# Gradient tail of a recurrent-memory layer: FFN gradients placed between attention halves, memory blocks fetched ahead and turned in spread steps

## The chip, the cores and the metric

The kernel runs on one core of one Trainium2 chip. The metric is device time in microseconds (us) of one execution. Before the change three timed runs had a median of 3459.89 us (3448.79 to 3468.05). Engines are called as the profile calls them: TensorE or PE (matmuls and transposes), DVE and ACT (copies and packs), POOL and SP (here the two queues that issue transfers).

## The reference

A layer with two parts is run forward and backward: a recurrent attention, where 64 segments of 32 tokens pass 8 memory rows to one another, and a gated FFN. The outputs are the layer's result and nine gradients, all in bf16.

```python
h  = x + A(layernorm(x), mem0, Wq, Wk, Wv, Wo)    # 64 segments in sequence, 16 heads of 256
h2 = h + B(layernorm(h), w_gate, w_up, w_down)    # (silu(x w_gate) * (x w_up)) w_down
# returned: h2 and the gradients by x, mem0, Wq, Wk, Wv, Wo, w_gate, w_up, w_down
```

The kernel runs a forward chain, an FFN phase, a backward chain and then a **tail**, which multiplies stored activations with stored gradients to get the weight gradients. Only the tail is changed: first Wo (called O here), then six **units** for Wv, Wk, Wq by two halves (v0, v1, k0, k1, q0, q1), and DGP (w_gate), DU (w_up) and Z (w_down).

## The kernel before

Most of what the tail loads goes tile by tile into a ring of 33 slots of 4 KB per partition, handed out in turn:

```python
def ring():
    ri[0] += 1
    return slots[(ri[0] - 1) % len(slots)]
```

A unit needs 20 blocks of 128 rows. 16 are X tiles, loaded by transposing DMA on the queue of SP. 4 hold the memory rows: fetched on the queue of POOL into one buffer `ld`, packed by DVE and ACT into one buffer `pk`, turned by TensorE.

```python
def load_x(nm, hf):
    for t in range(NT):                         # 16
        x_t = ring()
        nc.sync.dma_start_transpose(out=x_t..., in_=dr["X_" + nm][t]...)
def load_m(nm, hf):
    for g in range(NG):                         # 4
        nc.gpsimd.dma_start(out=ld, in_=dr["M_" + nm]...)
        nc.vector.tensor_copy(out=pk[:, 0:8], in_=ld...)
        nc.scalar.copy(out=pk[:, 8:16], in_=ld...)
        x_t = ring()
        for q in range(2):                      # 8 transposes each, then k.evac(x_t...)
            ...
```

A unit makes two passes over its 20 blocks; the next unit's memory blocks are made in one go between them.

```python
nxt = load_m("v", 0)
for hi, (nm, oi, hf) in enumerate(halves):
    xt = load_x(nm, hf)
    xt.update(nxt)
    for q in range(2):
        d_by_e(lambda b: HC[:, b, :], rhs, NB, (512, 512), st)
        if q == 0 and hi + 1 < len(halves):
            nxt = load_m(halves[hi + 1][0], halves[hi + 1][2])
GO = A(0, NB, D)                                # takes the place of HC
# load GO; then DGP, then DU, then Z (the only one that reads GO)
```

HC, HN and GO are operands kept whole outside the ring: HC for the six units, HN for DGP and DU, GO (the gradient of the output) for Z.

## Time and profile before

| stretch of the trace before | us |
|---|---|
| before the tail | 2713.3 |
| O | 135.0 |
| six attention units, DGP, DU | 530.3 |
| Z and the end | 50.9 |
| the tail, from O's first matmul on | 716.2 |
| span | 3429.5 |

Each stretch begins with the first matmul of its part. "Z and the end" begins with the start of the last matmul before Z, so that a wait of Z counts to Z. The view of who waited for whom, TensorE alone, over the six units (columns: engine, tile and line, what it waited for; us in total, times, longest):

```profile
PE ph L925 <- DVE arA L919: 15.5, 11, 6.5
PE psf L945 <- DMA arW<-X_k: 7.1, 4, 2.8
PE psf L945 <- DMA arW<-X_v: 4.1, 3, 1.7
PE psf L945 <- DMA arW<-X_q: 2.1, 2, 1.6
PE psf L945 <- DMA arA<-X_k: 1.2, 2, 0.7
PE psf L945 <- DMA arA<-X_q: 1.0, 1, 1.0
```

The first row is the wait of the transposes for a pack, the other five (15.5 us too) are waits for X tiles. Together 31.0 us.

### The profile page before, as it was taken

How to read it: one execution, taken by the hardware profiler on the slowest of the kernel's cores; microseconds unless marked ns; L12 is line 12 of the kernel's file. 1: busy time of each engine (PE TensorE's matmuls, PEld its weight loads, DVE VectorE, ACT ScalarE, POOL GpSimd, SP SyncE). 2: the span in 40 equal slices, each digit the busy share in tenths (PEclk: the TensorE clock that was granted, in tenths of full speed). 3: DMA queues.
4: the chain of work that ended last, by engine and by line, in shares of the span. 5: the costliest groups of instructions: out<-in, count | busy, mean ns of one | idle time of the engine just before them, and what ended most of it. 6: DMA issues, size and time to landing. Idle time of an engine off the chain costs nothing.

```text
span 3429.5 us, 120857 instructions
## 1 busy us (share of the span) xinstructions
PE 3044.6 (89%) x55036; PEld 2058.0 (60%) x55046; DVE 1308.3 (38%) x2912; ACT 971.0 (28%) x2171; POOL 616.2 (18%) x1293
## 2 busy tenths in 40 slices
PE   5999999999999578882999999999999899999999
PEld 4777777777777355661666666666666454443444
DVE  4444444444444256670444444444444201111101
ACT  1333333333333223330333333333333202111100
POOL 2111111111111111111122121212221111111111
PEclk8999999999999899995999999999999899999999
DMA  7545433644544787899688777878787969888571
GB/s 263 155 133 149 155 125 128 174 136 131 148 139 134 196 189 176 185 210 229 142 159 178 164 168 157 177 161 165 166 177 163 308 195 209 175 173 173 155 249 38
DMA packets 994213, 583.65 MB, mean 170 GB/s; under 512 B 904564, under 2 KB 913108, under 8 KB 992100
## 3 DMA queue, kind: packets, MB, share of 16 engines
q1 hardware_dynamic: 925748, 340.37, 47.6%
q0 software_dynamic: 67952, 235.56, 20.6%
q8 instruction: 430, 7.05, 0.9%
q14 instruction: 83, 0.68, 0.1%
HBM read 104.05 MB, written 250.19 MB: 103 GB/s over the span
## 4 chain that ended last, share of the span: by engine, by line
PE 61%; issue 13%; DMA 10%; DVE 8%; SPq 4%; ACT 2%; POOL 2%; ACTq 0%; DVEq 0%; POOLq 0%
PE psf L385 12%; PE po L780 7%; PE psf L422 5%; PE psf L737 5%; PE psf L945 4%; PE psf L715 4%; PE po L460 3%; PE fx L486 3%; PE fx L839 3%; PE psf L560 2%; SPq L910 2%; PE psf L802 2%; DVE arA L75 2%; PE psf L469 2%; DMA arW<-in_A_Wo_dram 2%
## 5 line engine op out<-in xcount | busy, mean ns | idle before, releaser
L77 ACT CAST arA<-psf 128x320 bf16<-128x320 f32 (+4 forms) x1139 | 487.0, 447 | 1611.8 <-PE psf L385 449.5
L75 DVE CAST arA<-psf 128x384 bf16<-128x384 f32 (+6 forms) x1029 | 491.7, 495 | 1085.1 <-PE psf L945 363.3
L385 PE MATMUL psf<-arA,arW 128*128 128x40 bf16 x16384 | 434.9, 181 | 34.3 <-issue 13.1
L385 PEld LDWEIGHTS <-arW 128*128 128x128 bf16 x16384 | 432.7, 97 | 49.6 <-issue 26.9
L780 PE MATMUL po<-arW,arA 128*32 128x448 bf16 x6144 | 355.2, 362 | 46.9 <-DMA arW<-in_A_Wv_dram 25.5
L737 PE MATMUL psf<-arA,arW 128*128 128x40 bf16 x8192 | 219.6, 180 | 51.3 <-POOL arA L672 41.1
L945 PE MATMUL psf<-arW,arA 128*128 128x512 bf16 x990 | 252.7, 383 | 13.4 <-DMA arW<-X_k 7.1
L422 PE MATMUL psf<-arW,arA 128*64 128x512 bf16 x2048 | 260.5, 383 | 2.4 <-DMA arW<-in_A_Wv_dram 2.4
L737 PEld LDWEIGHTS <-arW 128*128 128x128 bf16 x8192 | 215.3, 96 | 71.1 <-issue 70.6
L780 PEld LDWEIGHTS <-arA 128*32 128x32 bf16 x6144 | 155.2, 98 | 163.1 <-issue 35.2
L945 PEld LDWEIGHTS <-arA 128*128 128x128 bf16 x1440 | 135.4, 98 | 189.3 <-issue 44.7
L560 PE MATMUL psf<-arA,arW 128*128 128x256 bf16 x1344 | 166.1, 286 | 82.3 <-DMA arA<-arA 48.6
L560 PEld LDWEIGHTS <-arW 128*128 128x128 bf16 x1344 | 137.3, 102 | 113.5 <-issue 85.8
L422 PEld LDWEIGHTS <-arA 128*64 128x64 bf16 x2048 | 147.2, 111 | 70.3 <-issue 3.5
L75 DVE CAST arB<-psf 40x320 bf16<-40x320 f32 x320 | 107.7, 336 | 98.7 <-PE psf L451 65.0
L715 PEld LDWEIGHTS <-arW 128*128 128x128 bf16 x2048 | 87.9, 101 | 66.4 <-issue 62.7
L77 ACT CAST arB<-psf 128x96 bf16<-128x96 f32 (+1 forms) x320 | 98.2, 307 | 104.2 <-DVE arB L75 51.7
L486 PE MATMUL fx<-arW,arA 128*128 128x448 bf16 x512 | 124.5, 353 | 0.0
L747 ACT COPY arA<-psf 128x1024 bf16<-128x1024 bf16 x128 | 123.4, 1015 | 3.2 <-PE psf L746 1.7
L460 PE MATMUL po<-arW,arB 128*8 128x448 bf16 x2048 | 110.8, 359 | 9.0 <-DMA arW<-in_A_Wo_dram 5.4
L715 PE MATMUL psf<-arB,arW 128*128 128x80 bf16 x2048 | 98.7, 203 | 17.3 <-DVE arB L764 7.7
L966 PE MATMUL psf<-arW 128*128 128x448 bf16 x450 | 95.4, 361 | 5.8 <-DMA arW<-X_o 5.7
(238 smaller groups left out, 3741.8 us busy)
## 6 DMA issues: line engine op xcount, KB each, us to landing
QT<-arA POOLq DMA_DIRECT2D x64, 512.0 KB, 4.1
KT<-arA SPq DMA_DIRECT2D x64, 512.0 KB, 3.4
VG<-arA SPq DMA_DIRECT2D x64, 512.0 KB, 3.1
X_o<-arA POOLq DMA_DIRECT2D x40, 512.0 KB, 4.3
X_v<-arA POOLq DMA_DIRECT2D x32, 512.0 KB, 6.5
X_k<-arA POOLq DMA_DIRECT2D x32, 512.0 KB, 4.0
X_q<-arA POOLq DMA_DIRECT2D x32, 512.0 KB, 4.3
arW<-X_o SPq DMA_DIRECT2D x30, 512.0 KB, 13.7
```

The costliest lines, as they stand in the source:

```text
L75: nc.vector.tensor_copy(out=out, in_=in_)
L77: nc.scalar.copy(out=out, in_=in_)
L385: nc.tensor.matmul(pss[b][:, jj * L:(jj + 1) * L], lhsT=W_sb[:, kc, c * P:(c + 1) * P], rhs=hT_roll[:, kc, sl, :], start=(kc == 0), stop=( ...
L422: nc.tensor.matmul(pV[b][64 * g:64 * g + 64, 0:512], lhsT=hT_flat[:, kc, sl * L:sl * L + 64], rhs=Wv_sb[:, kc, n * 512:(n + 1) * 512], sta ...
L460: nc.tensor.matmul(pO[32 * (j % 4):32 * (j % 4) + M, 0:D], lhsT=o8[:, j, :], rhs=Wo_sb[:, cj(j), :], start=(j < 4), stop=(j >= MC - 4), sk ...
L486: nc.tensor.matmul(px[:, 0:D], lhsT=xblk[:, j, :], rhs=Wo_sb[:, cj(j), :], start=(j == 0), stop=(j == MC - 1))
L560: nc.tensor.matmul(ps[:, f2 * 256:(f2 + 1) * 256], lhsT=Wt[:, kc, c * P:(c + 1) * P], rhs=xT[:, kc, :], start=(kc == 0), stop=(kc == KC - 1))
L715: nc.tensor.matmul(ps[b][:, i * 2 * L:(i + 1) * 2 * L], lhsT=lhs[:, cl, :], rhs=rhs_bd[:, cl // 2, :, :].rearrange("p g n -> p (g n)"), st ...
L737: nc.tensor.matmul(pss[b][:, jj * L:(jj + 1) * L], lhsT=WoT_sb[:, kc, c * P:(c + 1) * P], rhs=do_roll[:, kc, sl, :], start=(kc == 0), stop ...
L747: nc.scalar.copy(out=dO_sb[:, 8 * hf:8 * hf + 8, :], in_=ph.rearrange("p (c n) -> p c n", n=P))
L780: nc.tensor.matmul(pH[32 * (j % 4):32 * (j % 4) + 32, 0:D], lhsT=blk[nm][:, j, r * SEG:(r + 1) * SEG], rhs=WT[:, cj(j), :], start=(nm == " ...
L945: nc.tensor.matmul(pa[2 * kc + g][:, 0:w], lhsT=lhs_of(b)[:, kc * P:(kc + 1) * P], rhs=rhs_of(b, g), start=(b == 0), stop=(b == nblk - 1), ...
```

## The change

Its intent is that TensorE never waits in the units. (1) Two `ld` and two `pk` buffers. (2) Fetch, pack and turn become separate steps, hung into the unit's own first pass four blocks apart, with two fetches in the pass before. (3) DGP after v0 and DU after k0. (4) A unit's X tiles now take their slots before its memory blocks; this follows from (2). In the cut below f, p and t with a number are the fetch, the pack and the turn of memory block 0 to 3.

```diff
-    ld = A(33.5, 4, 16, 32)
-    pk = A(37.5, 16, 4, 32)
+    ld_b = [A(33.5, 4, 16, 32), B(0, 4, 16, 32)]
+    pk_b = [A(37.5, 16, 4, 32), B(4, 16, 4, 32)]
...  load_m now returns a list of (fetch, pack, turn); in d_by_e:
         for b0 in range(0, nblk, 4):
+            for fn in (at or {}).get(b0, ()):
+                fn()
...  in att(hi, mem, after):
         xt = load_x(nm, hf)
-        xt.update(nxt)
+        for g in range(NG):
+            xt[NT + g] = ring()
...
+            if q == 0:
+                at = {0: [p0, f2], 4: [lambda: t0(xt[NT]), p1, f3], 8: [lambda: t1(xt[NT + 1]), p2],
+                      12: [lambda: t2(xt[NT + 2]), p3], 16: [lambda: t3(xt[NT + 3])]}
+            elif after is not None:
+                at = {12: [after[0][0], after[1][0]]}
...
+    for hi in range(len(halves)):
+        att(hi, mems[hi], mems[hi + 1] if hi not in (0, 2) else None)
+        if hi == 0:
+            up_grad("DGP", 7, mems[1])
+        if hi == 2:
+            up_grad("DU", 8, mems[3])
+    GO = A(0, NB, D)          # loaded here, and Z follows at once
```

More of the change, by code (lines that the diff above doesn't have):

```diff
@@ L914, in load_m, with fetch, pack, turn @@
     def load_m(nm, hf):
-        tiles = {}
+        todo = []
         for g in range(NG):
-            nc.gpsimd.dma_start(out=ld, in_=dr["M_" + nm][g * 4:(g + 1) * 4].rearrange(
-                "s p (c m) -> p s c m", m=32)[:, :, hf * 16:(hf + 1) * 16, :])
-            nc.vector.tensor_copy(out=pk[:, 0:8], in_=ld[:, :, 0:8, :].rearrange("p s c m -> p c s m"))
-            nc.scalar.copy(out=pk[:, 8:16], in_=ld[:, :, 8:16, :].rearrange("p s c m -> p c s m"))
-            x_t = ring()
-            for q in range(2):
-                pt = k.ph1()
-                for i in range(8):
-                    nc.tensor.transpose(pt[:, i * P:(i + 1) * P], pk[:, 8 * q + i].rearrange("p s m -> p (s m)"), ident[:, :])
-                k.evac(x_t[:, q * 1024:(q + 1) * 1024], pt[:, 0:1024])
-            tiles[NT + g] = x_t
-        return tiles
+            def fetch(g=g, ld=ld_b[g % 2]):
+                nc.gpsimd.dma_start(out=ld, in_=dr["M_" + nm][g * 4:(g + 1) * 4].rearrange(
+                    "s p (c m) -> p s c m", m=32)[:, :, hf * 16:(hf + 1) * 16, :])
+            def pack(ld=ld_b[g % 2], pk=pk_b[g % 2]):
+                nc.vector.tensor_copy(out=pk[:, 0:8], in_=ld[:, :, 0:8, :].rearrange("p s c m -> p c s m"))
+                nc.scalar.copy(out=pk[:, 8:16], in_=ld[:, :, 8:16, :].rearrange("p s c m -> p c s m"))
+            def turn(x_t, pk=pk_b[g % 2]):
+                for q in range(2):
+                    pt = k.ph1()
+                    for i in range(8):
+                        nc.tensor.transpose(pt[:, i * P:(i + 1) * P], pk[:, 8 * q + i].rearrange("p s m -> p (s m)"), ident[:, :])
+                    k.evac(x_t[:, q * 1024:(q + 1) * 1024], pt[:, 0:1024])
+            todo.append((fetch, pack, turn))
+        return todo
     dcs = dr["DHb"].rearrange("(t p) d -> p t d", p=P)[:, :, 0:D]
@@ L935, in tail_phase, with d_by_e @@
     nc.gpsimd.dma_start(out=HC, in_=dr["HC"].rearrange("(t p) d -> p t d", p=P)[:, :, 0:D])
-    def d_by_e(lhs_of, rhs_of, nblk, widths, store):
+    def d_by_e(lhs_of, rhs_of, nblk, widths, store, at=None):
         pa = accs(7)
         for b0 in range(0, nblk, 4):
+            for fn in (at or {}).get(b0, ()):
+                fn()
             for b in range(b0, min(nblk, b0 + 4)):
@@ L985, in tail_phase, with att @@
     halves = [(nm, oi, hf) for (nm, oi) in (("v", 5), ("k", 4), ("q", 3)) for hf in range(2)]
-    nxt = load_m("v", 0)
-    for hi, (nm, oi, hf) in enumerate(halves):
+    def att(hi, mem, after):
+        nm, oi, hf = halves[hi]
         o2 = OUT[oi].rearrange("d h e -> d (h e)")
         xt = load_x(nm, hf)
-        xt.update(nxt)
+        for g in range(NG):
+            xt[NT + g] = ring()
         for q in range(2):
+            at = {}
+            if q == 0:
+                (f0, p0, t0), (f1, p1, t1), (f2, p2, t2), (f3, p3, t3) = mem
+                at = {0: [p0, f2], 4: [lambda: t0(xt[NT]), p1, f3], 8: [lambda: t1(xt[NT + 1]), p2],
+                      12: [lambda: t2(xt[NT + 2]), p3], 16: [lambda: t3(xt[NT + 3])]}
+            elif after is not None:
+                at = {12: [after[0][0], after[1][0]]}
             def st(kc, g, r, q=q, hf=hf, o2=o2):
@@ L997, in rhs, with up_grad @@
                 return xt[b].rearrange("p (cl g n) -> p cl g n", g=2, n=P)[:, 4 * q:4 * q + 4, g, :]
-            d_by_e(lambda b: HC[:, b, :], rhs, NB, (512, 512), st)
-            if q == 0 and hi + 1 < len(halves):
-                nxt = load_m(halves[hi + 1][0], halves[hi + 1][2])
-        if hi == 1:
-            nc.gpsimd.dma_start(out=HN[:, 0:NT, :], in_=dr["HN"].rearrange("(t p) d -> p t d", p=P))
-    GO = A(0, NB, D)
-    nc.gpsimd.dma_start(out=GO[:, 0:NT, :], in_=GO2.rearrange("(t p) d -> p t d", p=P))
-    for (nm, oi) in (("DGP", 7), ("DU", 8)):
+            d_by_e(lambda b: HC[:, b, :], rhs, NB, (512, 512), st, at)
+    def up_grad(nm, oi, after):
         xt = []
@@ L1020, in rhs @@
                 return xt[b][:, p0 + 512 * g:p0 + 512 * g + ws[g]]
-            d_by_e(lambda b: HN[:, b, :], rhs, NT, ws, st)
+            d_by_e(lambda b: HN[:, b, :], rhs, NT, ws, st, {8: [after[0][0], after[1][0]]} if p0 else None)
+    mems = [load_m(nm, hf) for (nm, _, hf) in halves] + [None]
+    mems[0][0][0]()
+    mems[0][1][0]()
+    for hi in range(len(halves)):
+        att(hi, mems[hi], mems[hi + 1] if hi not in (0, 2) else None)
+        if hi == 0:
+            nc.gpsimd.dma_start(out=HN[:, 0:NT, :], in_=dr["HN"].rearrange("(t p) d -> p t d", p=P))
+            up_grad("DGP", 7, mems[1])
+        if hi == 2:
+            up_grad("DU", 8, mems[3])
+    GO = A(0, NB, D)
+    nc.gpsimd.dma_start(out=GO[:, 0:NT, :], in_=GO2.rearrange("(t p) d -> p t d", p=P))
     zt = []
```

## The prediction

> **What bounds the kernel now.** The change touches only the tail, the last phase, which computes the weight gradients. So I first asked how much of the run the tail is, then how much of it is TensorE idling. The page (its heading, and its first part) gives the scale:
>
> ```profile
> span 3429.5 us, 120857 instructions
> PE 3044.6 (89%) x55036; PEld 2058.0 (60%) x55046; DVE 1308.3 (38%) x2912; ACT 971.0 (28%) x2171; POOL 616.2 (18%) x1293
> ```
>
> TensorE leads. The groups by line put the attention part of the tail (L925, L945, L950) from 2847.8 to 3288.9 us; then come the two FFN gradients (DGP, DU) to 3378 and the Z gradient to 3421.5. Everything before 2847.8, 83% of the run, keeps its code.
>
> The attention part is six units (v, k, q by two halves), each of two passes over 20 blocks. From the timeline of TensorE, four blocks are 24 matmuls of 512 columns every 0.2157 us (5.18 us) and eight narrow ones in 1.05 us: 6.27 us in steady state. A pass is five of these, 31.35 us. The turning of one unit's memory blocks is 64 transposes, eight in 0.45 us: 3.6 us. I cut the busy-time view at the pass borders (columns: stretch, its length, PE, PEld, DVE, ACT, POOL busy with counts, clock, DMA share, GB/s):
>
> ```profile
> 2847.80:2892.05 44.25, 37.75 (x225) 17.67 (x224) 6.98 (x13) 10.61 (x14) 6.67 (x11) 0.92 1.12 230
> 2930.08:2966.03 35.95, 31.81 (x162) 13.13 (x162) 2.57 (x4) 2.15 (x4) 4.27 (x9) 1.00 0.72 132
> 2966.03:3003.84 37.81, 35.94 (x225) 16.71 (x226) 6.85 (x12) 10.27 (x12) 7.48 (x13) 1.00 0.91 203
> 3077.70:3116.09 38.39, 34.29 (x162) 13.70 (x163) 2.57 (x4) 2.14 (x4) 4.27 (x9) 0.91 0.72 136
> 3226.30:3257.60 31.30, 31.30 (x161) 13.13 (x160) 2.57 (x4) 2.14 (x4) 4.24 (x9) 1.00 0.48 98
> ```
>
> The last pass shows the ideal, 31.3. Passes with transposes (counts of 225) should take 34.95. The twelve passes took 44.25, 38.03, 35.95, 37.81, 36.03, 37.83, 38.39, 37.81, 35.00, 37.40, 31.30 and 31.40: together 441.1 us, against 12 x 31.35 + 6 x 3.6 = 397.8. So 43.3 us are lost, and that is all this part has to give.
>
> There are two losers, and they fall in different passes. The six passes with transposes lose 9.3 + 3.1 + 2.9 + 2.9 + 2.9 + 2.4 = 23.4 us; four passes without them lose 4.6 + 4.7 + 7.0 + 3.6 = 19.9 us. The chain that ended last (start, length, what), in one of the first kind:
>
> ```profile
> 2969.05 1.06 ACT arA L920
> 2970.39 3.90 DMA arA<-M_k
> 2974.37 1.05 ACT arA L920
> 2975.71 4.43 DMA arA<-M_k
> 2980.23 0.44 DVE arA L919
> 2980.72 0.62 PE ph L925 x8
> ```
>
> One buffer holds the fetched block: the next fetch starts only after ACT has packed the last one, and four rounds of fetch (about 4 us) and pack (1 us) run in series while PE, which takes its instructions in order, has come to the transposes.
>
> For the second kind, the timeline of the queue of SP, which loads the X tiles (start, length of the run of issues, what):
>
> ```profile
> 2901.98 6.36 SPq L910 DMA_TRANSPOSE arW<-X_v  x2
> 2911.28 29.31 SPq L910 DMA_TRANSPOSE arW<-X_k  x9
> 2940.76 9.84 SPq L910 DMA_TRANSPOSE arW<-X_v  x4
> ```
>
> Unit v1 starts at 2930.1 and needs its last four X_v tiles by block 12, but nine tiles of the unit after it go first. The chain runs through these SP issues and a 5.66 us landing until 2951. I read the cause in the code: the ring has 33 slots, a unit takes 4 (memory blocks) and then 16 (X), so X tiles 9 to 12 of the next unit inherit the slots of this unit's memory blocks, read last of all. The tiles of the unit after that inherit slots free earlier and overtake. The last unit has no such loss: after it come plain, quick row loads.
>
> **What the Trainium skill says.** "Perfetto Trace Analysis", section Optimization Strategy, says that where the most-contended engine changes between regimes, interleaving them can help. The trace agrees that the regimes differ: DMA share is 0.72 to 1.12 in the stalled passes, 0.26 in DU and 0.12 in Z. "TensorE: Matmul & The Clock Gate", section Part 1, says an idle window of about 3.4 us halves the clock until some 3.4 us of work. The trace agrees in kind: after the 6.48 us wait at 2855.98 eight transposes took 1.03 us instead of 0.61, and the 10 us around it had a clock of 0.66. "DMA: Bandwidth & Descriptors", section Latency and other measured facts, gives DMA transposes 261 GB/s; 512 KB would be 2.0 us, my estimate, and the shortest issue in the trace is 2.03. Its section on issuing engines says that SP and POOL queues share the same 16 engines; the median M fetch takes 4.6 us to land but up to 14.9 in a full queue.
>
> **The change part by part.** No matmul, transpose, copy or byte is added or removed. The work of 397.8 + 89 (DGP and DU) + 43.5 (Z) us stays.
>
> 1. Memory blocks. There are two fetch and two pack buffers; blocks 0 and 1 are fetched at block 12 of the preceding pass, two groups of 6.3 us ahead; block 2 right after the first pack. Each fetch has about 12.5 us before its pack, which has 6.3 us before its transposes. Against 4.6 us to land and 1.05 us to pack, the wait goes. Of 23.4 us I leave 3: 2 for the first unit, whose fetches meet other loads, 1 for the rest. Gain 20.
>
> 2. Ring order and placement. X tiles now take slots before the memory blocks, so slots are handed on in the order in which they are read and nothing overtakes. Placing DGP after v0 and DU after k0 gives 44 us of PE work with light loads (16 plain row tiles of 448 KB) just where 16 transposes must arrive. With 13 slots ahead of a 20-slot unit, 13 X tiles of the next unit can start while this unit starts. At an observed 2.8 to 3.2 us each, 16 take about 50 us, inside a unit of 66.3. Of 19.9 us I leave 3. Gain 17.
>
> 3. New cost: the GO load. It overwrites HC, so it waits for the last attention unit's blocks 0 to 15, ends 6.3 us before that unit, and Z now follows at once (before, DGP and DU lay between). Its row in the view by source line:
>
> ```profile
> L1005 POOL DMA_DIRECT2D arA<-in_grad_out_dram x1: 1199/1199/1199, 3283.0 to 3283.0; - x1
> DMA to landing us min/median/max: 14.0/14.0/14.0
> ```
>
> Those 14 us were beside 15 DU loads (DMA share 0.92 to 1.02). The same-sized HN load took 9.9 us. With Zt already in, I take 9 to 10: PE waits about 3.5 us. Cost 3.5.
>
> 4. Everything else, 0: HN has 66 us of slack before DGP; the end after the last matmul (8 us) is unchanged.
>
> Sum: 20 + 17 - 3.5 = 33.5 us, 1.0% of 3459.89. Predicted: 3426 us.
>
> **Rivals.**
> - *GO becomes a real stall.* If it lands in 14 us again, PE idles 7.7 us and restarts at half clock, some 2 to 3 us more: about 3433. For it: 1.8 MB in one transfer with one completion. Against it: the DMA queue is nearly empty there.
> - *DMA is the true bound*, so the X waits only move. A pass pair 2930 to 3004 holds 35.95 x 0.72 + 37.81 x 0.91 = 60.3 us of DMA work, 91% of 66.3. If loads slip in k1, q0 and q1, which have no light part between them, 8 to 12 us of part 2 come back: about 3437. Against it: the share falls below 0.3 in 10 us slices of every such unit, so the limit was order and not rate.
> - *The queue order at build turns out badly.* Order on each engine is fixed and differs from the program's (transposes sit between matmuls now). If a pack or a fetch is placed where POOL or DVE waits on something late, stalls return: 3450 to 3470. A new overtaking on SP would do the same. Nothing in the profile shows it; the slack of 12 us speaks against it.
> - *Nothing remains at all*: both residues zero and GO hidden: 3417.
>
> **Range and chances.** The most there is to win is 43.3 us, 1.25%, so faster by over 2% would need time from phases the change does not touch. Slower by over 2% needs 69 us of new waits. The three times before spread from 3448.8 to 3468.1, so I add some 8 us of noise either way to 3417 to 3440: range 3408 to 3446. Chances: 0.02 faster, 0.96 same, 0.02 slower.
>
> **What would show it right or wrong.** Right: twelve attention passes near 31.4 or 35 us; no M fetch in the chain inside them; on SP no tile of a later unit ahead of an earlier unit's; DGP and DU still 44 to 45 us each; PE idle 2 to 5 us before the first Z matmul, waiting for the gradient-output load; a span shorter by about 33 us. Wrong: waits on X in units k1, q0 and q1 (DMA rate was the bound), waits of PE on packs (placement), or a Z wait over 7 us. A changed time before 2847.8 would mean that the earlier phases had moved, which I put at zero.

## The result

The changed kernel had a median of 3404.42 us (3398.78 to 3418.66, 4 runs), the kernel before 3454.92 (3448.79 to 3468.05, 4 runs). The ratio is 0.9855, 95% interval 0.9809 to 0.9901. (A ratio is the mean time of one kernel's runs over that of the other's of the same rounds, so not quite the ratio of the medians.) Within 2%, as forecast; but 3404.42 lies just under the forecast range of 3408 to 3446.

The profile after, heading and first part:

```profile
span 3397.0 us, 120843 instructions
PE 3040.2 (89%) x55036; PEld 2058.9 (61%) x55046; DVE 1307.9 (39%) x2912; ACT 969.1 (29%) x2171; POOL 615.3 (18%) x1293
```

The span is 32.5 us shorter than before with the same counts of matmuls and copies: no work went, only idle time. Who waited, TensorE alone, from the first unit to the end:

```profile
PE psf L972 <- DMA arA<-in_grad_out_dram: 5.4, 1, 5.4
PE psf L951 <- issue: 0.3, 2, 0.2
```

All six rows of before are gone and a new one stands there. The ends of the passes, read from DVE's evacuations (timeline of DVE; start, length, what, idle before it and its releaser):

```profile
3062.20 1.89 DVE L75 CAST arA<-psf 128x512 bf16<-128x512 f32 x3 [3.65 <-issue]
...
3093.55 1.89 DVE L75 CAST arA<-psf 128x512 bf16<-128x512 f32 x3 [28.60 <-PE psf L951]
...
3118.63 1.89 DVE L75 CAST arA<-psf 128x512 bf16<-128x512 f32 x3 [22.33 <-PE psf L951]
...
3138.90 1.88 DVE L75 CAST arA<-psf 128x512 bf16<-128x512 f32 x3 [17.52 <-PE psf L951]
```

From 3062.20 to 3093.55 is k0's second pass: 31.35 us, the ideal to the hundredth. The next two distances, 25.08 and 20.27, are DU's passes, and passes with transposes from v1 on take 34.9 to 35.2. Units, DGP and DU together took 489.3 us against an ideal of 12 x 31.35 + 6 x 3.6 + 2 x 45.35 = 488.5. SP's timeline shows the loads in unit order:

```profile
2892.99 47.45 SPq L910 DMA_TRANSPOSE arW<-X_v  x16
2947.42 9.02 SPq L910 DMA_TRANSPOSE arA<-X_k  x3
...
3088.65 29.45 SPq L910 DMA_TRANSPOSE arW<-X_k  x10
3125.62 26.37 SPq L910 DMA_TRANSPOSE arW<-X_q  x9
```

No X tile stands before one of an earlier unit. The new cost, before Z (timeline of TensorE):

```profile
3339.26 1.05 PE L956 MATMUL fx<-arW,arA 128*64 128x512 bf16 x8
3345.66 2.03 PE L972 MATMUL psf<-arA,arW 128*128 128x448 bf16 x5 [5.35 <-DMA arA<-in_grad_out_dram]
```

The same place in the trace of before, then POOL after the change:

```profile
3378.93 1.12 PE L966 MATMUL psf<-arA,arW 128*128 128x448 bf16 x5
```

```profile
3336.32 1.20 POOL L1045 DMA_DIRECT2D arA<-in_grad_out_dram  x1 [24.06 <-issue]
```

GO landed 9.2 us after its issue began. TensorE stood still for 5.35 us, and its first five matmuls took 2.03 us where five took 1.12 at the same place before. Z and the end grew from 50.9 to 57.1 us.

By stretch, after: 2714.2 before the tail, O 136.4, units with DGP and DU 489.3, Z and the end 57.1; tail 682.8. The tail is 33.4 us shorter. The forecast sum was 33.5. The medians of the timed runs differ by 50.5, though, and the experiments had to find out which of the two is the gain.

### The profile page after: what moved, and what is told of

It is laid out like the page before. It is cut to its first block, busy times and chain, and to the rows that moved or that the text cites.

```text
span 3397.0 us, 120843 instructions
## 1 busy us (share of the span) xinstructions
PE 3040.2 (89%) x55036; PEld 2058.9 (61%) x55046; DVE 1307.9 (39%) x2912; ACT 969.1 (29%) x2171; POOL 615.3 (18%) x1293
## 4 chain that ended last, share of the span: by engine, by line
PE 71%; DMA 8%; issue 8%; DVE 8%; SPq 2%; ACT 2%; POOL 1%; DVEq 0%; ACTq 0%; POOLq 0%
PE psf L385 12%; PE psf L951 8%; PE po L780 7%; PE psf L422 6%; PE psf L737 5%; PE psf L715 4%; PE po L460 3%; PE fx L486 3%; PE psf L972 3%; PE fx L839 3%; PE psf L560 3%; PE psf L802 2%; PE fx L956 2%; PE psf L469 2%; DVE arA L75 2%
## 5 line engine op out<-in xcount | busy, mean ns | idle before, releaser
L75 DVE CAST arA<-psf 128x384 bf16<-128x384 f32 (+6 forms) x1029 | 492.1, 495 | 1007.7 <-PE psf L385 322.8
L385 PEld LDWEIGHTS <-arW 128*128 128x128 bf16 x16384 | 432.2, 97 | 48.9 <-issue 26.5
L737 PEld LDWEIGHTS <-arW 128*128 128x128 bf16 x8192 | 216.2, 97 | 71.9 <-issue 71.5
L951 PE MATMUL psf<-arW,arA 128*128 128x512 bf16 x1030 | 259.5, 379 | 0.0
L951 PEld LDWEIGHTS <-arA 128*128 128x128 bf16 x1440 | 136.0, 98 | 164.8 <-issue 13.7
L560 PEld LDWEIGHTS <-arW 128*128 128x128 bf16 x1344 | 139.0, 104 | 113.3 <-issue 83.3
L75 DVE CAST arB<-psf 40x320 bf16<-40x320 f32 x320 | 107.8, 337 | 98.2 <-PE psf L451 65.0
L715 PEld LDWEIGHTS <-arW 128*128 128x128 bf16 x2048 | 88.0, 101 | 66.4 <-issue 63.5
L972 PEld LDWEIGHTS <-arW 128*128 128x128 bf16 x606 | 59.4, 100 | 76.0 <-DMA arW<-X_o 13.3
```

Of the source, the lines that this page charges most:

```text
L75: nc.vector.tensor_copy(out=out, in_=in_)
L385: nc.tensor.matmul(pss[b][:, jj * L:(jj + 1) * L], lhsT=W_sb[:, kc, c * P:(c + 1) * P], rhs=hT_roll[:, kc, sl, :], start=(kc == 0), stop=( ...
L560: nc.tensor.matmul(ps[:, f2 * 256:(f2 + 1) * 256], lhsT=Wt[:, kc, c * P:(c + 1) * P], rhs=xT[:, kc, :], start=(kc == 0), stop=(kc == KC - 1))
L715: nc.tensor.matmul(ps[b][:, i * 2 * L:(i + 1) * 2 * L], lhsT=lhs[:, cl, :], rhs=rhs_bd[:, cl // 2, :, :].rearrange("p g n -> p (g n)"), st ...
L737: nc.tensor.matmul(pss[b][:, jj * L:(jj + 1) * L], lhsT=WoT_sb[:, kc, c * P:(c + 1) * P], rhs=do_roll[:, kc, sl, :], start=(kc == 0), stop ...
L951: nc.tensor.matmul(pa[2 * kc + g][:, 0:w], lhsT=lhs_of(b)[:, kc * P:(kc + 1) * P], rhs=rhs_of(b, g), start=(b == 0), stop=(b == nblk - 1), ...
```

## Experiments

Twelve runs. A trace's tail is measured as above. This table has all of it; "pack" and "loads" are TensorE's waits in the units in that trace.

| run | median us | ratio to before (95%) | before the tail | units, DGP, DU | Z, end | tail | pack | loads |
|---|---|---|---|---|---|---|---|---|
| before, first trace | 3459.89 | | 2713.3 | 530.3 | 50.9 | 716.2 | 15.5 | 15.5 |
| before_again | 3441.63 | 1.0004 (0.9969-1.0040) | 2736.0 | 526.5 | 50.9 | 712.0 | 14.0 | 15.0 |
| before_third | 3434.78 | 0.9975 (0.9942-1.0008) | 2703.6 | 530.3 | 50.9 | 716.6 | 17.1 | 15.7 |
| changed, first trace | 3404.42 | 0.9855 (0.9809-0.9901) | 2714.2 | 489.3 | 57.1 | 682.8 | 0 | 0 |
| after_again | 3412.66 | 0.9928 (0.9890-0.9965) | 2721.1 | 489.3 | 57.8 | 686.0 | 0 | 0 |
| after_third | 3417.52 | 0.9920 (0.9886-0.9954) | 2739.2 | 489.2 | 57.1 | 682.1 | 0 | 0 |
| go_early | 3404.32 | 0.9889 (0.9851-0.9927) | 2729.2 | 489.3 | 50.8 | 677.9 | 0 | 0 |
| steps_only | 3405.28 | 0.9892 (0.9858-0.9925) | 2723.1 | 489.2 | 50.1 | 675.2 | 0 | 0 |
| steps_one | 3407.70 | 0.9885 (0.9848-0.9921) | 2726.0 | 499.6 | 50.4 | 684.7 | 0.5 | 0 |
| one_buffer | 3408.54 | 0.9890 (0.9826-0.9953) | 2720.8 | 489.3 | 53.7 | 678.1 | 0 | 0 |
| old_order | 3438.39 | 0.9975 (0.9914-1.0036) | 2728.7 | 519.8 | 50.1 | 706.7 | 0 | 22.5 |
| placed_only | 3452.20 | 1.0000 (0.9932-1.0068) | 2729.8 | 528.2 | 58.6 | 721.4 | 24.8 | 3.7 |
| ring_order (wrong results) | 3448.47 | 0.9988 (0.9913-1.0063) | 2740.9 | 533.8 | 50.9 | 719.6 | 20.9 | 0 |
| own_unit | 3452.71 | 1.0023 (0.9989-1.0056) | 2733.9 | 541.2 | 50.4 | 726.3 | 36.1 | 0 |

Two things can be read off at once. The column "before the tail" runs from 2703.6 to 2740.9 though that code is the same in every row. The column "tail" repeats within 4.6 us for the same kernel.

### How large is the gain? before_again, after_again, after_third, before_third

Edit: none.

> The kernel before, unchanged, against itself. It tests the question that the forecast left: the two profiles differ by 32.5 us, the medians of the timed runs by 50.5 us. Theory N (scatter of the phases before the tail, whose code is the same): ratio 1.000 with an interval that reaches at least 0.3% to either side, and in this second trace the tail (first matmul of the output-weight gradient to the end of the span) again takes 716 us within 3 us, with any difference of the span lying before it. Rival S (the tail of the kernel before is itself slower in most runs than in the one profile that I read, because its loads come late by luck): the tail in this trace is 5 us or more over 716, with more waits for X or M tiles.

> The changed kernel, unchanged, timed in five rounds. Theory N: the gain is that of the two profiles' tails, 716.2 - 682.8 = 33.4 us, ratio 0.990 within 0.002, tail again 683 us within 2 us. Rival S: the ratio stays at 0.985 to 0.987 and the tail of the kernel before is the longer by some 50 us.

> The changed kernel a third time, beside the smaller version in the same rounds. Theory N (the difference of the tails is the whole gain): tail 683 to 686, ratio to before 0.990 within 0.003, 5 to 9 us above the smaller version. The stretch from the end of the forward chain to the end of the FFN's matmuls, whose code no version changes, scatters again between 389 and 417 us.

> The kernel before, a third trace. Theory N: tail 712 to 717; everything else that differs lies in the same stretch of the FFN. Rival Y (the kernel before is slower there too, for a reason that the change removes): this trace has that stretch over 405 us and the third trace of the changed kernel has it under 400.

Most of the scatter lies before the tail. Against itself the kernel before gave 1.0004 and 0.9975. Its three tails were 716.2, 712.0 and 716.6, mean 714.9; those of the changed kernel 682.8, 686.0 and 682.1, mean 683.6. The difference is 31.3 us. My bounds were a little narrow: 712.0, 686.0 and 682.1 lie about 1 us outside them, and so does the ratio of after_again (0.9928, forecast 0.988 to 0.992). The forecast for after_third also missed in its last part: its tail was 2.6 us below that of the smaller version (steps_one), not 5 to 9 above. The stretch from the end of the forward chain to the end of the FFN's matmuls took 389.2 us in the first trace of before and 416.7 in the second. The busy-time view over just that stretch, first before_again, then before_third (391 us there):

```profile
1149.30:1566.00 416.70, 303.45 (x2185) 209.99 (x2182) 232.10 (x352) 112.44 (x196) 66.97 (x122) 0.88 0.89 185
```

```profile
1149.00:1540.00 391.00, 305.32 (x2183) 210.56 (x2180) 232.00 (x352) 112.53 (x195) 67.34 (x122) 0.90 0.88 197
```

Every engine's busy time agrees within 2 us; 25.7 us of idling differ. Most of it is one wait of the FFN's first matmuls for a DMA, at most 61.8 us in before_again against 44.0 in before_third:

```profile
PE psf L560 <- DMA arA<-arA: 68.1, 6, 61.8
```

```profile
PE psf L560 <- DMA arA<-arA: 47.3, 4, 44.0
```

Rival Y, that the kernel before is slower there as well, falls: its third trace had 391.0 in this stretch and the changed kernel's third had 411.0. In the fourteen traces this one wait took 42.0 to 61.8 us: 43.7, 61.8 and 44.0 in the kernel before, 42.0, 56.0 and 59.7 in the changed one. Why that transfer varies from run to run was not tried. The three ratios of the changed kernel, 0.9855, 0.9928 and 0.9920, have a mean of 0.9901, which is 34 us of the mean of before (45 runs on several chips: 3444.2 us, from 3421.9 to 3470.4, standard deviation 11.7). The mean of the changed kernel's 16 runs is 3414.3, 29.9 less. Timed runs and traced tails agree on 30 to 34 us, 0.9 to 1.0%.

### Is the wait for GO a cost with nothing behind it? go_early

```diff
         if hi == 2:
             up_grad("DU", 8, mems[3])
+            GO = W(0, NB, D)              # in the place of HN, which nothing reads after DU
+            # load GO here
-    GO = A(0, NB, D)
-    # load GO here
```

> The changed kernel with the gradient-output block put in the place of HN instead of HC, and loaded right after the DU gradient, so that Z need not wait for it. Theory (the 5.4 us wait before Z is a new cost of the change and has nothing behind it): that wait is 0, the slow-clock restart of Z (about 2 us more) is gone too, the tail is 7 us shorter than the changed kernel's 683, about 676, and the time 0.2% below the changed kernel's. Rival (the Zt loads or the PSUM hand-over wait as long behind it): the wait changes its name and the tail stays within 2 us of 683.

The wait is gone, Z and the end took 50.8 us again, and the tail was 677.9, which is 5.7 under the changed kernel's mean of 683.6 (forecast 7; O was 1.4 us longer here than in the first trace of the change). Nothing stood behind that wait.

### Does the placement earn anything? steps_only and placed_only

steps_only is the changed kernel with DGP and DU moved back behind the units:

```diff
-        att(hi, mems[hi], mems[hi + 1] if hi not in (0, 2) else None)
-        if hi == 0:
-            up_grad("DGP", 7, mems[1])
-        if hi == 2:
-            up_grad("DU", 8, mems[3])
+        att(hi, mems[hi], mems[hi + 1])
     GO = A(0, NB, D)
+    # load GO, then up_grad("DGP", 7), up_grad("DU", 8)
```

> The changed kernel without the placement: all six attention units first, then DGP, DU and Z as before; two buffers, spread steps and the new slot order stay. Theory O (the order in which ring slots are handed on was the cause of the X waits, and placement adds nothing): no X wait over 1 us in total, and, as the gradient-output load is hidden again behind DU, a tail 5 to 8 us shorter than the changed kernel's, about 676. Rival P (the light FFN loads between the units are what lets the X tiles arrive): X waits of 10 to 20 us return and the tail is 690 to 700.

Theory O held: no load was waited for, the units with DGP and DU took 489.2 us, and with GO hidden behind DGP again the tail was 675.2. So with the new slot order and the spread steps the placement earns nothing and costs the wait for GO.

placed_only is the kernel before with the placement alone; during DGP and DU the memory blocks for the next unit are made between their passes.

```diff
         for q in range(2):
             d_by_e(...)
-            if q == 0 and hi + 1 < len(halves):
+            if q == 0 and hi in (1, 3, 4):
                 nxt = load_m(...)
+        if hi == 0:
+            nxt = up_grad("DGP", 7, ("v", 1))     # load_m after its first pass
+        if hi == 2:
+            nxt = up_grad("DU", 8, ("k", 1))
```

> The kernel before with the placement alone: DGP after v0 and DU after k0, the next unit's memory blocks fetched, packed and turned in one go between the two passes of whatever comes before it, one buffer each, memory slots still ahead of X slots. In the queue of SP as built, three DGP tiles come after twelve X_v tiles and the last four X_k tiles of k0 come after thirteen DU tiles. Theory O: overtaking is only moved, X and FFN tile waits of 8 to 15 us stay, pack waits of 12 to 16 us stay, and the wait for the gradient-output block before Z (5 us and 2 of restart) is added: tail 712 to 722, no gain. Rival P (placement helps by itself): loads wait under 5 us, tail under 706.

The tail (721.4) fell in the range of Theory O, but not for its reason. The waits in this trace from the first unit to the end:

```profile
PE ph L925 <- DVE arA L919: 24.8, 12, 7.5
PE psf L966 <- DMA arA<-in_grad_out_dram: 6.3, 1, 6.3
PE psf L945 <- DMA arW<-X_q: 3.7, 3, 1.6
```

Placement does cure most of the X waits (3.7 us instead of 15), as Rival P said. But the waits for packs rose from about 15 to 24.8 and took nearly all of it back: the units with DGP and DU took 528.2 us against a mean of 529.0 before. What made the tail 6.5 us longer than before is the wait for GO (Z and the end 58.6 us instead of 50.9). M_v fetches landed at a median of 8.6 us instead of 6.0; the two that grew most were issued at 2880.5 and 2890.3 us, beside the plain rows of DGP. What made them late was not tested.

### The two waits one at a time: ring_order, own_unit and old_order

ring_order was to be the new slot order alone:

```diff
+    slot = [ring() for _ in range(NB)]            # 16 for X, then 4 for memory, ahead of each unit
-            x_t = ring()                          # in load_x
+            x_t = got[t]
-            x_t = ring()                          # in load_m
+            x_t = got[NT + g]
```

> The kernel before with one thing changed: a unit's ring slots are handed out to its 16 X tiles first and to its 4 memory blocks after them. Buffers, steps and placement are those of before. In the queue of SP as built, no tile of a later unit now stands before one of an earlier unit. Theory O (handing on of slots caused the X waits): TensorE's waits on X tiles fall from about 15 us (with the pauses around them 20) to under 2, its waits on packs stay at 14 to 16, and the tail falls from 712 to 716 to about 694. Rival R (the rate of the transposing loads was the limit): X waits stay over 8 us and the tail over 703.

Its results were wrong (relative error 0.31, 0.45 and 0.41 in the gradients of Wq, Wk and Wv). With this order the memory blocks of the next unit inherit slots of X tiles 3 to 6 of the running unit, and in program order they are written between its two passes, before the second one reads those tiles. The kernel before cannot have the better order as long as it turns the blocks between the passes. Its loads keep their sizes, so the X waits may still be read: they were 0. But five waits on evacuations (5.5 us) come from the false dependence, so its tail settles nothing.

own_unit has the order with right results, by making the memory blocks at the start of their own unit:

```diff
-    nxt = load_m("v", 0)
...
         xt = load_x(nm, hf)
-        xt.update(nxt)
+        xt.update(load_m(nm, hf))
...
-            if q == 0 and hi + 1 < len(halves):
-                nxt = load_m(...)
```

> The order of the slots alone, this time with right results: the kernel before, with the fetch, pack and turn of a unit's memory blocks moved to the start of that unit, so that its X tiles take their slots first. One buffer each, all four blocks in one go, FFN gradients at the end. The queue of SP as built is in unit order. Theory C (the two waits cover for each other: the pack rounds lengthen when the X loads no longer stop for them): waits on X tiles under 2 us, waits on packs 20 to 30 us instead of 14 to 15.5, tail 706 to 720, so the order alone wins less than 10 of the 40 us. Rival A (the two are separate terms, 20 us each, as I had forecast): waits on packs stay at 14 to 16 us and the tail falls to about 694.

```profile
PE ph L925 <- DVE arA L919: 36.1, 7, 8.7
```

That is its only row of waits in the units. X waits are 0, as they should be if the slot order was their cause; but X tiles could also land during the long waits for packs, so it takes old_order, below, to show it. The waits for packs are 36.1 us, over the 20 to 30 of Theory C, and the tail is 726.3, which is 11.4 us worse than before and over its 706 to 720. One part stays open: this run also moves the burst to where X loads run, and moved burst and changed order can't be told apart in it.

old_order is the reverse: steps_only with memory slots ahead of X slots again, so SP's queue is that of before tile for tile, while steps and buffers are new.

```diff
-        tiles = {}                                # in load_x
+        tiles = {NT + g: ring() for g in range(NG if nm != "o" else 0)}
...
-        for g in range(NG):                       # in att
-            xt[NT + g] = ring()
```

> The changed kernel without the placement, and with memory slots handed out ahead of X slots as in before; the queue of SP as built is then that of before, tile for tile. Two buffers and spread steps stay. Theory O: waits on packs stay at 0 and the X waits of before return, 12 to 16 us of waits and about 20 with the pauses: tail about 695, that is 20 more than the 675.2 of the run without placement. Rival R2 (X loads are late only because they share the engines with badly timed memory fetches): X waits under 5 us, tail under 682.

```profile
PE psf L951 <- DMA arW<-X_k: 10.7, 5, 3.9
PE psf L951 <- DMA arW<-X_v: 7.0, 2, 6.3
PE psf L951 <- DMA arA<-X_q: 2.7, 2, 2.0
PE psf L951 <- DMA arA<-X_k: 1.3, 2, 0.9
PE psf L951 <- DMA arW<-X_q: 0.8, 1, 0.8
```

No wait for packs is left, and the X waits are 22.5 us where before had 15.5. I had expected 12 to 16 and a tail of 695; it was 706.7. The slot order alone, with everything else equal, is worth 706.7 - 675.2 = 31.5 us. The spread steps without it are worth 714.9 - 706.7 = 8.2 us.

### Is the second buffer needed? one_buffer and steps_one

```diff
-    ld_b = [A(33.5, 4, 16, 32), B(0, 4, 16, 32)]
-    pk_b = [A(37.5, 16, 4, 32), B(4, 16, 4, 32)]
+    ld_b = [A(33.5, 4, 16, 32)] * 2
+    pk_b = [A(37.5, 16, 4, 32)] * 2
...
-  at = {0: [p0, f2], 4: [t0, p1, f3], 8: [t1, p2],     12: [t2, p3], 16: [t3]}   # lambdas left out
+  at = {0: [p0, f1], 4: [t0, p1, f2], 8: [t1, p2, f3], 12: [t2, p3], 16: [t3]}
# and only block 0 is fetched in the pass before
```

> The changed kernel with a single fetch buffer and a single pack buffer; block 0 is fetched ahead, and each further fetch goes out with the pack before it, one group (6.3 us) ahead of its own pack. Theory T (the spread of the steps over the pass is what counts; 6.3 us cover 4.6 us of landing): no wait on packs over 1 us in all, tail 683 to 687 as in the changed kernel. Rival B (the second buffer is needed, as 4.6 us is a median and some fetches take twice that): pack waits of 5 to 15 us, tail 690 to 698.

With the placement one buffer is enough: no wait for packs, units with DGP and DU 489.3 us, tail 678.1. It even came in under the changed kernel's 683.6: in this trace GO was waited for only 3.4 us and no spell of half clock followed (Z and the end 53.7 us instead of 57.3), and O was 1.9 us shorter.

steps_one is one_buffer without the placement.

> What the runs so far point to as the least that does it all: slot order and spread steps, one fetch and one pack buffer, no placement. Theory: no wait on packs, X tiles or the gradient-output block over 1 us; tail 675 to 678, 7 us under the changed kernel, as in the run without placement. Rival: with one buffer the fetches of the back-to-back units meet more X loads than with the placement and pack waits of 3 to 10 us appear, tail 680 to 686.

The rival's size was right (684.7; the units took 10.4 us longer), its name was not. No pack held up the transposes for long. The timeline of DVE around the place:

```profile
2956.00 0.69 DVE L75 COPY arW<-ph 128x1024 bf16<-128x1024 bf16 x1 [5.44 <-PE ph L929]
2968.28 0.43 DVE L922 COPY arA<-arA 128x1024 bf16<-128x1024 bf16 x1 [11.59 <-DMA arA<-M_k]
2968.62 1.88 DVE L75 CAST arA<-psf 128x512 bf16<-128x512 f32 x3
```

A pack for the next unit stood in DVE's queue ahead of the evacuation of the finished pass. Its fetch was late: it was issued at 2952.4, once the one buffer was free, and landed 15.8 us later (in steps_only, with two buffers, the same fetch was issued at 2936.1 and landed after 5.5). DVE started the evacuation only after that pack, and so TensorE waited 6.7 us for the evacuation (row "PE psf L951 <- DVE arA L75") and restarted slowly (five matmuls in 2.41 us, later five in 1.24). In this trace, then, the second buffer, or the placement, does count. It is one trace: in the timed runs steps_one was not slower than the changed kernel of its rounds (3407.70 against 3417.52).

### A version that beats both

steps_only gave the shortest tail: 675.2 us, 8.4 under the changed kernel's mean and 39.7 under that of before. In the same rounds its median was 3405.28 against 3412.66 for the changed kernel, with ratios to before of 0.9892 and 0.9928. The intervals overlap, so it is the tails that carry this, and steps_only has one trace. go_early, with the placement kept, is its equal within the scatter (677.9).

## Why the prediction was wrong, and where it was right

**The step that failed** is the last one, "Range and chances": the level that the sum was taken from, and "some 8 us of noise either way". The prediction took 33.5 us off 3459.89, the median of three runs. That level was 15.7 us over the mean of 45 runs, 3444.2; 3444.2 - 33.5 = 3410.7, and the changed kernel's 16 runs have a mean of 3414.3. The scatter of one kernel is some 24 us to either side, and medians of 3 to 11 runs of the kernel before went from 3434.78 to 3459.89. (The range's own sum slipped as well: 8 us on either side of 3417 to 3440 is 3409 to 3448.) The sign of it lay open: the profiled run was 3431.3 us, 28.6 below that median and outside the three runs' spread, and I used its rows without using its time. The four runs of the result then fell low, at 3404.42: that both groups strayed, and in opposite directions, was bad luck.

**The sum was right, its terms were not.** Forecast 33.5, traced 33.4 in the first pair and 31.3 over three traces each; that it came so close was partly luck.
- *Part 1, packs (20) and part 2, X tiles (17).* Together they gave 714.9 - 675.2 = 39.7 us, against 37 forecast; the 6 us of residue that I left were 0. But as separate terms they don't exist: the steps without the order gave 8.2, the order without the steps -11.4 (own_unit, which also moves the burst), and the placement, which I counted into part 2, -6.5 by itself, all of it the wait for GO. At least in one direction the two waits hide one another: without waits for packs, X waits rose from 15.5 to 22.5 us (old_order). With the X waits gone, packs were waited for 20.9 us (ring_order, wrong results) and 36.1 us (own_unit) instead of 15.5; what part the order had in that is not shown. The terms came from sorting the lost time of one trace by pass: that tells where time was lost, not what one would win by removing one cause.
- *Ring order as the cause* was right and is shown by old_order against steps_only: 31.5 us, one trace each, where the tails of one kernel repeat within 4.6.
- *Placement* was credited with helping the X tiles. In the changed kernel it earns 0 (489.3 against 489.2) and brings the GO wait.
- *Part 3, GO (3.5).* Landing 9 to 10 us was right (9.2). TensorE waited 5.35, as POOL issued the load at 3336.3, 2.3 us after the blocks that it waits for were done, for no cause that the profile shows. The slow restart, which I put only into a rival, came on top: 6.2 us in all.
- *Part 4, everything else 0*: shown; what moved before the tail moved just as much between two traces of the same kernel.

**The skill's points.** "Perfetto Trace Analysis", section Optimization Strategy, on interleaving regimes: I read the trace as agreeing, and the runs disagree. The regimes do differ, but once the order was right there was no gap left for interleaving to fill. "TensorE: Matmul & The Clock Gate", Part 1, on the slow clock after idling: seen again after the GO wait (2.03 us for five matmuls instead of 1.12). The prediction's comparison of its 2.0 us estimate with the shortest issue shows little: that is the time of an issue on SP, not of a landing, and the shortest among the X loads of that trace is 2.01 us, not 2.03.

## What to carry to other kernels

In a ring of buffers the order in which slots are handed out is also the order in which loads may start: give first to what is read first, or a later consumer's load overtakes an earlier one's. Two waits that recur in the same loop may cover each other; a term per wait can have the right sum and still tell you nothing of what either fix earns alone. And before forecasting one percent, compare the profiled run's own time with the timed ones: here the unchanged part scattered by as much as the change was worth.

## What the Trainium skill lacked or had wrong

- "Perfetto Trace Analysis", Optimization Strategy, advises to find the gaps and remove their causes, and names interleaving of regimes. It has no warning that gaps hide one another (8.2 us for the steps alone, -11.4 in own_unit, 39.7 together), and interleaving alone left the units, DGP and DU at 528.2 us against 529.0 here.
- "Perfetto Trace Analysis", the same section, names too few buffers as what repeated gaps can mean, and not the order in which they are handed out. Here the same 33 slots in another order removed 31.5 us, and a second fetch buffer made no difference where the placement stood (489.3 us both ways).
- "DMA: Bandwidth & Descriptors", on issuing engines that share the 16 DMA engines, gives no size for it. Fetches of 512 KB landed after 3.7 to 17.2 us in these traces.
- "TensorE: Matmul & The Clock Gate", Part 1, puts the idle window at about 3.4 us and calls it free-running. The clock record of own_unit agrees with the second: its spells of half clock begin at 2880.47, 2958.98, 3037.48, 3115.99, 3187.67 and 3259.35 us, and the distances (78.5 and 71.7) are 23 and 21 times 3.413. But a pause need not fill 3.4 us: one of 2.92 us was followed by half clock (eight transposes in 1.03 us). After one of 3.95 us the first eight were still fast (0.62) and half clock began 0.5 us later; after the 3.40 us before Z in one_buffer none followed.
- No page looked up has run-to-run scatter of a single-core kernel: 3421.9 to 3470.4 us for the same kernel. Between two of its traces one DMA wait of 44.0 or 61.8 us made 17.8 of the 25.7 us in which that phase differed.
